# Attention and two MLP layers on one core: ten ticks per attention unit, three slots per column block, two column blocks begun early, all operands at one residue modulo 512 bytes

## The chip, the cores and the metric

The kernel runs on one core of one Trainium2 chip. The core has TensorE (PE in the profile; its weight loads are PEld), VectorE (DVE), ScalarE (ACT), GpSimd (POOL) and SyncE (SP, here only a queue for DMAs), the on-chip memory SBUF and eight PSUM banks of 128 partitions by 512 fp32 values, into which TensorE writes. The metric is the time on the device in microseconds (us), as a median over runs. Besides it there is a profile of one execution, with each instruction's start and end.

## The reference

It computes attention over 2 x 8 heads (768 positions, 64 values a head) with 4 sink positions and a window of 128, then two MLP layers on the 1536 tokens of width 512 with 2048 hidden columns.

```python
keep = is_sink | in_window
scores = np.where(keep, scale * np.matmul(q, k.transpose(0, 1, 3, 2)), -1000000000.0)
a = np.exp(scores - np.max(scores, axis=-1, keepdims=True))
a = a / (np.sum(a, axis=-1, keepdims=True) + 1e-09)
x = np.matmul(a, v)                         # -> (1536, 512)
...
r = np.maximum(x @ w_in, 0.0)               # first layer
x = (r * r) @ w_out
...
h = x @ w_in                                # second layer
P = a[0] + a[1]*h + a[2]*h*h + a[3]*h*h*h
Q = 1.0 + np.abs(b[0])*np.abs(h) + np.abs(b[1])*h*h
return (P / (Q + 1e-06)) @ w_out
```

## The kernel before

The tokens stand in four groups: 512, 256, 256 and 512 columns (GROUPS; 0 to 3). The hidden width of 2048 is worked in 16 column blocks f of 128. Every operand of a large product is split into two parts, hi and lo, and a product is three matmuls: hi by hi, hi by lo, lo by hi. So the first GEMM of a block is 4 x 3 = 12 matmuls (`gemm1`, L437 to L439, tiles xhi, xlo, whi, wlo), and the second is 8 with ghi (L460, L461; "hi matmuls" below) and 4 with glo (L464; "lo matmuls"). In the second layer the lines are L437 to L439 and L495 to L497, with yhi and ylo in place of xhi and xlo for the token tiles 0 and 2; tile 1 takes the buffers of xhi and xlo again.

Between the two GEMMs of the first layer stands `act1`: a Relu and two squares on ACT (L446 to L448) and the residual glo on DVE (L449), all in the PSUM bank that the first GEMM wrote; the bank is free when glo has been formed. The second GEMM of block f - 2 follows the first GEMM of block f (LAG = 2).

The weights come as 64-bit floats, 512 KB a load. A conversion (`w_split_`) is a cast to `top` on ACT (L134), a merge to `wt` on DVE (L135), the cast whi on ACT (L421) and the residual wlo on DVE (L422). There is one `top` buffer.

Attention works in units of two heads and two blocks of 128 positions: eight units for each of groups 0 and 3, four for each of groups 1 and 2. A unit is a generator (`att_unit`): two steps with scores (L302, "QK"; each needs two banks, whose contents DVE reduces and masks at L308, tiles p and mn, and ACT exponentiates at L310), then the sums and the normalization (L313 to L318), some empty steps, the transposes (L335, "TR", two banks, copied by ACT and DVE into pT), the sink transposes (L347, "TRs", copied by ACT into pS), then the sink products and PV (L358, L370) and a copy of the result.

The head of the program runs the eight units of group 0 one behind the other, with CONV[k] conversions at step k, and begins HEAD column blocks of the first GEMM in banks of their own as soon as a quarter of x is there. Then `group(g)` runs the layer's 16 blocks for group g, and lets the attention of group g + 1 go on beside it: `slot(k)` stands at two places in each f and calls `tick()` as often as an even spread of nt ticks asks. A tick starts a new unit if the tick's number is a multiple of PER, and moves every unit under way by one step, the new one first. In group 0 the attention has banks 6 and 7 alone, in groups 1 and 2 four banks; the first GEMM uses 4 and 5, and the second GEMM of group 0 holds 0 to 3.

TensorE's order in the head and in groups 0 to 2 is as the code writes it (`manual_schedule`); the order of the other engines, and TensorE's elsewhere, is set by a scheduler when the program is built. Each engine works through its queue in order.

Of the kernel before, what the change touches and what calls it, by code (L numbers as in the profile page):

```python
# [10 lines left out]
F32 = mybir.dt.float32  # L11
# [8 lines left out]
P = 128  # L20
# [5 lines left out]
NF = DFF // P  # L26
NC = DM // P
# [10 lines left out]
YEVAC_ACT = (0, 1)  # L38
PINNED = (0, 1, 2)
NUNIT = (4, 4, 8)  # L40
CONV = (1, 1, 1, 1, 1, 2, 2, 2, 2)
PER = 4
HEAD = 3
DEPTH = 4
NALT = 4
LAG = 2
# [1 line left out]
TAIL = 3  # L48
HP = 60
NTOP = 1  # L50
PAD = 128
IAD = 3
ST_T = 2
ST_PV = 1
TG2 = 512
GN = [sum(s[2] for s in g) * P for g in GROUPS]
# [100 lines left out]
class Fast:  # L157
# [17 lines left out]
    def setup(self):  # L175
        nc, c = self.nc, self.const
        self.zero = c.tile([P, P], BF16, name="zero")
        nc.gpsimd.memset(self.zero, 0.0)
        self.tops = [c.tile([P, WH], I32, name=f"top{i}") for i in range(NTOP)]
        self.conv_i = 0  # L180
        for top in self.tops:
            nc.gpsimd.memset(top, 0)
        self.ident = c.tile([P, P], F32, name="ident")
        self.nsw = c.tile([P, 4], I32, name="nsw")
        self.nswf = c.tile([P, 4], F32, name="nswf")
        self.par = c.tile([P, 2], F32, name="par")
        ab = c.tile([P, 6], F32, name="ab")
        self.ab = ab
        io = self.io
        nc.scalar.dma_start(self.nsw, io["nsw"].bitcast(I32).partition_broadcast(P))  # L190
        nc.scalar.dma_start(ab[:, 0:4], io["a"].partition_broadcast(P))
        nc.scalar.dma_start(ab[:, 4:6], io["bb"].partition_broadcast(P))
        make_identity(nc, self.ident)
        rel = self.wp.tile([P, WH], F32, tag="whi4_0", name="rel")[:, :P]
        col = self.wp.tile([P, WH], F32, tag="wlo4_0", name="col")[:, :P]
        nc.gpsimd.iota(rel, pattern=[[-1, P]], base=0, channel_multiplier=1,
                       allow_small_or_imprecise_dtypes=True)
        nc.gpsimd.iota(col, pattern=[[1, P]], base=0, channel_multiplier=0,
                       allow_small_or_imprecise_dtypes=True)
        v = nc.vector  # L200
        f = self.nswf
        t = c.tile([P, 2], F32, name="neg")
        v.tensor_copy(f, self.nsw)
        lo = f.rearrange("p (s w) -> p s w", w=2)[:, :, 0:1]
        hi = f.rearrange("p (s w) -> p s w", w=2)[:, :, 1:2]
        t3 = t.rearrange("p (s w) -> p s w", w=1)
        p3 = self.par.rearrange("p (s w) -> p s w", w=1)
        v.tensor_scalar(t3, lo, 0.0, 4294967296.0, op0=ALU.is_lt, op1=ALU.mult)
        v.tensor_tensor(t3, t3, lo, op=ALU.add)
        v.scalar_tensor_tensor(p3, in0=hi, scalar=4294967296.0, in1=t3, op0=ALU.mult, op1=ALU.add)  # L210
        ns, win = self.par[:, 0:1], self.par[:, 1:2]
        self.m0 = c.tile([P, P], F32, name="m0")
        self.m1 = c.tile([P, 2 * P], F32, name="m1")
        self.m2 = c.tile([P, 2 * KB], F32, name="m2")
        self.nabs = c.tile([P, 2], F32, name="nabs")
        m0, m1, m2 = self.m0, self.m1, self.m2
        tmp = lambda tag: self.wp.tile([P, WH], F32, tag=tag, name="tmp")[:, :P]
        out, fut, rel1 = tmp("whi4_1"), tmp("wlo4_1"), tmp("whi5_0")
        v.tensor_scalar(fut, rel, 0.0, -BIG, op0=ALU.is_lt, op1=ALU.mult)
        v.tensor_scalar_add(rel1, rel, 128.0)  # L220
        cur, prv = m2[:, KB : KB + P], m2[:, NSK:KB]
        v.tensor_scalar(cur, rel, win, -BIG, op0=ALU.is_ge, op1=ALU.mult)
        v.tensor_tensor(cur, cur, fut, op=ALU.min)
        v.tensor_scalar(out, col, ns, -BIG, op0=ALU.is_ge, op1=ALU.mult)
        v.tensor_tensor(m0, cur, out, op=ALU.max)
        v.tensor_scalar(prv, rel1, win, -BIG, op0=ALU.is_ge, op1=ALU.mult)
        v.tensor_tensor(m1[:, 0:P], prv, out, op=ALU.max)
        v.tensor_copy(m1[:, P : 2 * P], cur)
        v.tensor_copy(m2[:, :NSK], out[:, :NSK])
        v.tensor_copy(m2[:, KB + P :], out[:, :NSK])  # L230
        nu = 2 * sum(u[2][2] for u in units())
        self.mn = c.tile([P, nu], F32, name="mn")
        self.mn_i = 0
        c.tile([P, PAD // 4], F32, name="pad")


    def alt_tags(self, alt):
# [211 lines left out]
        nc.vector.tensor_tensor(glo, r, ghi.bitcast(F32), op=ALU.subtract)  # L449
        return ghi, glo  # L450

    def gemm2a(self, f, gg, n, acc):
        nc = self.nc
        ghi, glo = gg
        whi, wlo = self.w[(0, f, 1)]
        pk = n <= 256
        kw = dict(skip_group_check=True) if pk else {}
        for m in range(NC):
            ms = slice(m * P, (m + 1) * P)
            nc.tensor.matmul(acc[m], whi[:, ms], ghi, start=(f == 0 and not pk), stop=pk, **kw)  # L460
            nc.tensor.matmul(acc[m], wlo[:, ms], ghi, start=False, stop=pk, **kw)  # L461
        for m in range(NC):
            ms = slice(m * P, (m + 1) * P)
            nc.tensor.matmul(acc[m], whi[:, ms], glo, start=False, stop=pk or f == NF - 1, **kw)  # L464
# [35 lines left out]
    def run(self, ctx):  # L500
# [119 lines left out]

        self.att_banks = [2, 3, 6, 7, 1]
        self.new_x(0)
        hb = [self.bank(k) for k in (4, 5, 0)]
        pc = 0
        dh = []
        per = n0 // NC
# [29 lines left out]
        urgent = True  # L656
        acc, gs, ys, ysp = None, {}, {}, {}

        def second(which, g, f):
            nonlocal acc  # L660
            if f == 0 and which == 0 and GN[g] <= 256:
                bk = [self.bank(k) for k in range(2)]
# [7 lines left out]
            gg = gs.pop((which, g, f))  # L670
            if which == 0:
                n = GN[g]
                self.gemm2a(f, gg, n, acc)
                if f == NF - 1:
                    k = 0 if g == NG - 1 else g
                    y = self.yp.tile([P, self.yw[k]], F32, tag=f"y{k}", name="y")
                    if g == 2:
                        self.yx = y
                    y = y[:, : NC * n].rearrange("p (m n) -> p m n", m=NC)
                    for m in range(NC):  # L680
                        (A.copy if m % 2 == 0 or g in YEVAC_ACT else V.tensor_copy)(y[:, m], acc[m])
                    ys[g] = y
            else:
                self.gemm2b(f, gg, acc)
                if f == NF - 1:
                    for t in range(TG2 // P):
                        if g == NT2 - 1:
                            if t == 0:
                                ot = self.xp.tile([P, 4, DM], F32, tag="xhi", name="ot")
                            o = ot[:, t]  # L690
                        else:
                            o = self.stage.tile([P, DM], F32, tag="wt", name="o", bufs=2)
                        r0 = g * TG2 + t * P
                        dst = self.io["out"][r0 : r0 + P, :]
                        if g == NT2 - 1 and t == TG2 // P - 1:
                            A.copy(o[:, : DM // 2], acc[t][:, : DM // 2])
                            nc.scalar.dma_start(dst[:, : DM // 2], o[:, : DM // 2])
                            V.tensor_copy(o[:, DM // 2 :], acc[t][:, DM // 2 :])
                            nc.sync.dma_start(dst[:, DM // 2 :], o[:, DM // 2 :])
                        else:  # L700
                            (A.copy if t % 2 == 0 else V.tensor_copy)(o, acc[t])
                            nc.sync.dma_start(dst, o)
# [4 lines left out]
        def group(g):  # L707
            nonlocal sp, acc, pos, nt
            n = GN[g]
            last = g == NG - 1  # L710
            if last:
                assert done == len(us)
                sa.close()
                sp = ExitStack()
                self.ysp = mk(sp, "ysp", 1, "right")
                self.cp = self.ysp
                self.flag()
                wload(1, 3)
                nt = 0
            else:  # L720
                nt = PER * NUNIT[g] + 5
            self.att_banks = [6, 7] if n > 256 else [2, 3, 6, 7]
            pos = 0

            def slot(k):
                nonlocal pos
                while pos < min(nt, nt * (k + 2) // (2 * NF)):
                    tick()
                    pos += 1

            for f in range(NF):
                if g == 0 and f < HEAD:
                    h = hb[f]
                else:
                    h = self.gemm1(0, f, *self.x[g], n)
                gs[(0, g, f)] = self.act1(h, n)
# [1 line left out]
                    wconv(0, f + 4, 0)  # L738
                if last and f > 0:
                    wconv(1, f - 1, 0)  # L740
                slot(2 * f + 1)
                if f >= LAG:
                    second(0, g, f - LAG)
                if g == 0 and f + 1 < NF:
                    wconv(0, f + 1, 1)
                if last:
                    if f >= 3:
                        wconv(1, f - 3, 1)
                    if f in (4, 6, 8, 10):
                        with ExitStack() as cc:  # L750
                            cc.enter_context(tc.issue_after(self.lastX.ins))
                            self.split_y(0, (f - 4) // 2, ys, ysp)
                slot(2 * f + 2)
            if not last:
                while done < gdone[g + 1]:
                    tick()
# [255 lines left out]
```

## Time and profile before

| what | before |
|---|---|
| median of 3 runs | 679.44 us (678.81 to 680.25) |
| profiled execution, its own time | 680.43 us |
| its span, first to last instruction | 678.7 us |
| PE busy | 635.6 us, 94% |
| DVE busy | 424.8 us, 63% |
| ACT busy | 426.8 us, 63% |
| mean granted clock | 0.978 of full |

The head with group 0's attention runs to about 66 us, group 0 to 180, group 1 to 251, group 2 to 321 and group 3 to 405; the second layer then runs to 669. PE's busy time counts overlapping matmuls once, so 100% in a stretch means that it had a matmul in flight all the time, and not that the matmuls were as dense as they can be; how dense they are is read from their starts. A row's "idle before" is the time in which an engine had nothing in flight, with the instruction that ended it.

### The profile page before, as it was taken

How to read it: one execution, taken by the hardware profiler on the slowest of the kernel's cores; microseconds unless marked ns; L12 is line 12 of the kernel's file. 1: busy time of each engine (PE TensorE's matmuls, PEld its weight loads, DVE VectorE, ACT ScalarE, POOL GpSimd, SP SyncE). 2: the span in 40 equal slices, each digit the busy share in tenths (PEclk: the TensorE clock that was granted, in tenths of full speed). 3: DMA queues.
4: the chain of work that ended last, by engine and by line, in shares of the span. 5: the costliest groups of instructions: out<-in, count | busy, mean ns of one | idle time of the engine just before them, and what ended most of it. 6: DMA issues, size and time to landing. Idle time of an engine off the chain costs nothing.

```text
span 678.7 us, 9985 instructions
## 1 busy us (share of the span) xinstructions
PE 635.6 (94%) x3681; PEld 515.5 (76%) x3681; DVE 424.8 (63%) x849; ACT 426.8 (63%) x912; POOL 111.8 (16%) x122
## 2 busy tenths in 40 slices
PE   5668699999999999999999999999999999999994
PEld 2445467677788888899888888888888888888883
DVE  6885465543233354423666649999788887877772
ACT  4875566654455465546677758787676666766661
POOL 2111000000001011102000001353223332222221
PEclk9788699999999999999999999999999999999998
DMA  8870354432012122100455530000010000100001
GB/s 291 318 235 26 104 189 148 150 111 91 24 34 73 44 70 86 43 9 1 153 188 188 190 120 2 0 1 0 1 63 1 1 0 1 46 17 2 0 1 67
DMA packets 20794, 52.39 MB, mean 77 GB/s; under 512 B 2688, under 2 KB 8064, under 8 KB 20736
## 3 DMA queue, kind: packets, MB, share of 16 engines
q1 hardware_dynamic: 20160, 51.52, 22.3%
q8 instruction: 31, 0.51, 0.3%
q14 instruction: 27, 0.22, 0.1%
q10 hardware_dynamic: 576, 0.14, 0.1%
HBM read 48.50 MB, written 3.15 MB: 76 GB/s over the span
## 4 chain that ended last, share of the span: by engine, by line
PE 87%; ACT 6%; DVE 4%; issue 1%; DMA 1%; POOL 0%; POOLq 0%
PE b L437 13%; PE b L439 13%; PE b L438 13%; PE b L460 7%; PE b L461 7%; PE b L464 6%; PE b L496 6%; PE b L495 6%; PE b L497 6%; PE b L302 3%; ACT p L310 2%; PE b L370 2%; PE b L335 2%; ACT top L134 1%; PE b L358 1%
## 5 line engine op out<-in xcount | busy, mean ns | idle before, releaser
L437 PE MATMUL b<-xhi,whi 128*128 128x512 f32 (+1 forms) x320 | 113.7, 356 | 0.0
L439 PE MATMUL b<-xhi,wlo 128*128 128x512 f32 (+1 forms) x320 | 111.0, 347 | 0.0
L438 PE MATMUL b<-xlo,whi 128*128 128x512 f32 (+1 forms) x320 | 110.9, 347 | 0.0
L460 PE MATMUL b<-ghi,whi 128*128 128x512 f32 (+1 forms) x256 | 84.4, 346 | 6.6 <-DVE glo L449 6.6
L461 PE MATMUL b<-ghi,wlo 128*128 128x512 f32 (+1 forms) x256 | 82.9, 340 | 0.0
L486 POOL TENSOR_TENSOR glo<-t,ghi 128x512 fp32r<-128x512 f32 x34 | 45.0, 1324 | 215.3 <-ACT ghi L485 192.3
L449 DVE TENSOR_TENSOR glo<-b,ghi 128x512 fp32r<-128x512 f32 (+1 forms) x64 | 35.6, 556 | 71.2 <-ACT b L448 71.0
L496 PE MATMUL b<-wlo,ghi 128*128 128x512 f32 x192 | 74.9, 390 | 0.0
L310 ACT ACTIVATE p<-p,mn 128x288 f32<-128x288 f32 (+2 forms) x96 | 48.4, 505 | 41.6 <-DVE mn L308 41.4
L495 PE MATMUL b<-whi,ghi 128*128 128x512 f32 x192 | 74.5, 390 | 0.0
L497 PE MATMUL b<-whi,glo 128*128 128x512 f32 x192 | 72.0, 389 | 0.0
L318 POOL TENSOR_SCALAR p<-p,sums 128x288 f32<-128x288 f32 (+1 forms) x48 | 28.4, 602 | 260.8 <-DVE sums L314 179.7
L437 PEld LDWEIGHTS b<-xhi,whi 128*128 128x128 f32 x320 | 60.4, 189 | 10.3 <-issue 2.8
L439 PEld LDWEIGHTS b<-xhi,wlo 128*128 128x128 f32 x320 | 60.5, 189 | 7.7
L438 PEld LDWEIGHTS b<-xlo,whi 128*128 128x128 f32 x320 | 60.5, 189 | 7.2
L446 ACT ACTIVATE b<-b 128x512 f32<-128x512 f32 (+1 forms) x64 | 30.7, 482 | 54.9 <-PE b L439 54.7
L422 DVE TENSOR_TENSOR wlo<-wt,whi 128x512 fp32r<-128x512 f32 x64 | 45.0, 704 | 31.3 <-ACT whi L421 30.9
L308 DVE CUSTOM_DVE_ANT_0 p<-b,m 128x288 f32<-128x288 f32 (+2 forms) x96 | 37.0, 420 | 43.8 <-PE b L302 43.7
L421 ACT CAST whi<-wt 128x512 fp32r<-128x512 f32 x64 | 39.5, 617 | 31.5 <-PE b L438 21.0
L460 PEld LDWEIGHTS b<-ghi,whi 128*128 128x128 f32 x256 | 49.0, 191 | 13.1 <-DVE glo L449 7.0
L464 PE MATMUL b<-glo,whi 128*128 128x512 f32 (+1 forms) x256 | 55.6, 340 | 0.0
L461 PEld LDWEIGHTS b<-ghi,wlo 128*128 128x128 f32 x256 | 49.1, 192 | 5.1
(126 smaller groups left out, 1289.3 us busy)
## 6 DMA issues: line engine op xcount, KB each, us to landing
st<-w SPq DMA_DIRECT2D x64, 512.0 KB, 4.1
raw<-att SPq DMA_DIRECT2D x12, 400.0 KB, 3.1
rawv<-att SPq DMA_DIRECT2D x16, 192.0 KB, 2.7
raws<-att SPq DMA_DIRECT2D x16, 128.0 KB, 2.7
out<-o SPq DMA_DIRECT2D x8, 256.0 KB, 2.0
raw_e<-att SPq DMA_DIRECT2D x4, 400.0 KB, 5.4
raw<-att SPq DMA_DIRECT2D x6, 256.0 KB, 3.2
rawv<-att SPq DMA_DIRECT2D x8, 128.0 KB, 3.3
```

The costliest lines, as they stand in the source:

```text
L310: self.lastA = A.activation(p, p, AF.Exp, scale=-1.0, bias=mn, accum_out=sums[:, k * nb + i : k * nb + i + 1])
L422: nc.vector.tensor_tensor(wlo, t, whi.bitcast(F32), op=ALU.subtract)
L437: nc.tensor.matmul(h[:, :n], whi[:, cs], xhi[:, c, :n], start=(c == 0), stop=False)
L438: nc.tensor.matmul(h[:, :n], whi[:, cs], xlo[:, c, :n], start=False, stop=False)
L439: nc.tensor.matmul(h[:, :n], wlo[:, cs], xhi[:, c, :n], start=False, stop=(c == NC - 1))
L460: nc.tensor.matmul(acc[m], whi[:, ms], ghi, start=(f == 0 and not pk), stop=pk, **kw)
L461: nc.tensor.matmul(acc[m], wlo[:, ms], ghi, start=False, stop=pk, **kw)
L464: nc.tensor.matmul(acc[m], whi[:, ms], glo, start=False, stop=pk or f == NF - 1, **kw)
L486: self.lastL = nc.gpsimd.tensor_tensor(glo, t3, ghi.bitcast(F32), op=ALU.subtract)
L495: nc.tensor.matmul(acc[t], ghi[:, ts_], whi, start=(f == 0), stop=False)
L496: nc.tensor.matmul(acc[t], ghi[:, ts_], wlo, start=False, stop=False)
L497: nc.tensor.matmul(acc[t], glo[:, ts_], whi, start=False, stop=(f == NF - 1))
```

## The change

The tables of numbers:

```diff
-CONV = (1, 1, 1, 1, 1, 2, 2, 2, 2)
-PER = 4
-HEAD = 3
+CONV = (1, 1, 1, 1, 1, 1, 1, 1, 1)
+PER = 5
+HEAD = 2
...
-PAD = 128
...
-ST_T = 2
+ST_T = 5
...
-        c.tile([P, PAD // 4], F32, name="pad")
```

A unit now has three more empty steps between its normalization and its transposes (ST_T), a new one starts every fifth tick, and the head holds 9 conversions instead of 13. The removed tile of 128 bytes stood in the first pool, so every pool on the left side of SBUF moves down by 128 bytes. In the program of before the tiles whi, wlo, xhi, xlo, ghi and glo start at 96 modulo 512, and yhi and ylo, in a pool on the right side, at 480; in the changed program all of them start at 480.

The second GEMM and the slots:

```diff
-    def gemm2a(self, f, gg, n, acc):
+    def gemm2a(self, f, gg, n, acc, between):
...
+        if between:
+            between()
         for m in range(NC):
             ms = slice(m * P, (m + 1) * P)
             nc.tensor.matmul(acc[m], whi[:, ms], glo, start=False, stop=pk or f == NF - 1, **kw)
...
-        hb = [self.bank(k) for k in (4, 5, 0)]
+        hb = [self.bank(k) for k in (4, 5)]
...
-                nt = PER * NUNIT[g] + 5
+                nt = PER * NUNIT[g] + 6
...
             def slot(k):
                 nonlocal pos
-                while pos < min(nt, nt * (k + 2) // (2 * NF)):
+                first = 6 if g == 0 else -2
+                while pos < min(nt, nt * (k - first) // (3 * NF - first - 2)):
                     tick()
                     pos += 1
...
+                elif g == 0 and f == HEAD:
+                    h = self.bank(6)
+                    for c in range(NC):
+                        self.gemm1_part(0, f, c, self.x[0], n, h)
                 else:
                     h = self.gemm1(0, f, *self.x[g], n)
                 gs[(0, g, f)] = self.act1(h, n)
...
-                slot(2 * f + 1)
+                slot(3 * f + 1)
                 if f >= LAG:
-                    second(0, g, f - LAG)
+                    second(0, g, f - LAG, lambda: slot(3 * f + 2))
+                else:
+                    slot(3 * f + 2)
...
-                slot(2 * f + 2)
+                slot(3 * f + 3)
```

The new slot stands between the hi and the lo matmuls of the second GEMM. In group 0 the first tick falls on the eighth slot (f = 2), so no unit of group 1 starts in the head any more.

TensorE from the end of the head into group 0, before. L437 to L439 are the last quarter of the three column blocks in banks b4, b5 and b0, L460 is the first matmul of the second GEMM, L302 a QK burst of group 1's first unit:

```order
L302 MATMUL b6_784<-raw_700 64x288 x2
L302 MATMUL b7_785<-raw_700 64x288 x2
L437 MATMUL b4_150<-xhi_148,whi_192 128x512
L437 MATMUL b5_151<-xhi_148,whi_242 128x512
L437 MATMUL b0_152<-xhi_148,whi_308 128x512
L438 MATMUL b4_150<-xlo_149,whi_192 128x512
L439 MATMUL b4_150<-xhi_148,wlo_193 128x512
L438 MATMUL b5_151<-xlo_149,whi_242 128x512
L439 MATMUL b5_151<-xhi_148,wlo_243 128x512
L438 MATMUL b0_152<-xlo_149,whi_308 128x512
L439 MATMUL b0_152<-xhi_148,wlo_309 128x512
L460 MATMUL b0_814<-ghi_763,whi_451 128x512
```

The same place after (L345 is the sink transpose, L356 the sink product, L435 to L437 the first GEMM, L458 and L464 the hi and lo matmuls, L300 QK):

```order
L345 MATMUL b2_678<-ident_104,p_600 128x128 x2
L435 MATMUL b6_725<-xhi_147,whi_306 128x512
...
L356 MATMUL b2_678<-pS_681,raws_468 64x128 x4
...
L435 MATMUL b4_149<-xhi_147,whi_190 128x512
L435 MATMUL b5_150<-xhi_147,whi_240 128x512
L435 MATMUL b6_725<-xhi_147,whi_306 128x512
...
L437 MATMUL b6_725<-xhi_147,wlo_307 128x512
L458 MATMUL b0_753<-ghi_713,whi_446 128x512
...
L300 MATMUL b6_768<-raw_662 64x288 x2
L300 MATMUL b7_769<-raw_662 64x288 x2
L464 MATMUL b0_753<-glo_714,whi_446 128x512
```

The third column block has moved from b0 to b6, nine of its matmuls stand ahead of the sink products, and the QK bursts have left the head; the first stands between hi and lo.

TensorE in group 0, before: a QK burst of one unit and the transposes of another (L335) in the same tick, on the same two banks, after a lo matmul and ahead of the next first GEMM:

```order
L464 MATMUL b3_817<-glo_764,whi_451 128x512
L302 MATMUL b6_832<-raw_782 64x288 x2
L302 MATMUL b7_833<-raw_782 64x288 x2
L335 MATMUL b6_842<-ident_104,p_770 128x128 x4
L335 MATMUL b7_849<-ident_104,p_770 128x128 x4
L437 MATMUL b4_858<-xhi_148,whi_376 128x512
```

After, two blocks f in a row (L333 are the transposes):

```order
L437 MATMUL b4_909<-xhi_147,wlo_645 128x512
L300 MATMUL b6_939<-raw_778 64x288 x2
L300 MATMUL b7_940<-raw_778 64x288 x2
L458 MATMUL b0_753<-ghi_806,whi_787 128x512
...
L459 MATMUL b3_756<-ghi_806,wlo_788 128x512
L300 MATMUL b6_959<-raw_778 64x288 x2
L300 MATMUL b7_960<-raw_778 64x288 x2
L464 MATMUL b0_753<-glo_807,whi_787 128x512
...
L333 MATMUL b6_1018<-ident_104,p_766 128x128 x4
L333 MATMUL b7_1025<-ident_104,p_766 128x128 x4
L458 MATMUL b0_753<-ghi_873,whi_854 128x512
```

Each piece now stands alone, with at least the eight hi matmuls between it and the next on the same banks.

## Rows read from the trace of the kernel before

**Rows 1.** The page: the chain that ended last, shares of the span.

```profile
PE 87%; ACT 6%; DVE 4%; issue 1%; DMA 1%; POOL 0%; POOLq 0%
```

**Rows 2.** Busy time by stretch: window, its length, engines' busy us (instructions), clock, DMA.

```profile
72.90:78.30 5.40, 5.40 (x12) 3.79 (x12) 1.83 (x3) 1.02 (x2) 0.00 (x0) 0.50 0.57 193
78.30:180.60 102.30, 95.94 (x539) 73.62 (x539) 48.31 (x108) 58.38 (x127) 5.72 (x8) 1.00 0.35 116
251.00:320.80 69.80, 69.51 (x627) 61.48 (x626) 26.64 (x87) 37.88 (x112) 8.97 (x13) 1.00 0.13 40
```

**Rows 3.** Waits of PE from 66 to 180 us: total us, times, longest.

```profile
PE b L460 <- DVE glo L449: 6.6, 1, 6.6
PE b L335 <- DVE mn L308: 4.2, 7, 0.8
PE b L347 <- DVE mn L308: 2.2, 4, 0.6
```

**Rows 4.** Timeline of PE at group 0's start: start, us, line, operands, count, idle before.

```profile
65.89 0.39 PE L439 MATMUL b<-xhi,wlo 128*128 128x512 f32 x1
72.89 0.80 PE L460 MATMUL b<-ghi,whi 128*128 128x512 f32 x1 [6.61 <-DVE glo L449]
...
78.31 0.87 PE L302 MATMUL b<-raw 64*64 64x288 f32 x8
```

**Rows 5.** Timeline of ACT in the same wait.

```profile
67.90 0.58 ACT L447 ACTIVATE ghi<-b 128x512 fp32r<-128x512 f32 x1
...
68.89 0.59 ACT L447 ACTIVATE ghi<-b 128x512 fp32r<-128x512 f32 x1
```

**Rows 6.** Timeline of DVE: the third glo.

```profile
72.14 0.69 DVE L449 TENSOR_TENSOR glo<-b,ghi 128x512 fp32r<-128x512 f32 x1 [0.24 <-ACT b L448]
```

**Rows 7.** Timeline of PE at the end of the head.

```profile
60.78 0.38 PE L347 MATMUL b<-ident,p 128*128 128x128 f32 x2
...
61.74 0.66 PE L358 MATMUL b<-pS,raws 128*64 128x128 f32 x8
...
63.20 0.72 PE L302 MATMUL b<-raw 64*64 64x288 f32 x8
63.91 0.98 PE L437 MATMUL b<-xhi,whi 128*128 128x512 f32 x3
```

**Rows 8.** The chain that ended last, from 40 to 52 us: start, us, what.

```profile
43.51 0.78 ACT top L134
...
47.97 0.67 DVE wlo L422
```

**Rows 9.** Timeline of PE around one tick of group 0.

```profile
85.41 1.07 PE L464 MATMUL b<-glo,whi 128*128 128x512 f32 x4
86.40 0.72 PE L302 MATMUL b<-raw 64*64 64x288 f32 x8
87.68 0.44 PE L347 MATMUL b<-ident,p 128*128 128x128 f32 x2 [0.56 <-DVE mn L308]
87.87 0.48 PE L437 MATMUL b<-xhi,whi 128*128 128x512 f32 x1
88.19 0.39 PE L438 MATMUL b<-xlo,whi 128*128 128x512 f32 x1
```

**Rows 10.** Timeline of PE at group 2's start.

```profile
252.91 0.66 PE L358 MATMUL b<-pS,raws 128*64 128x128 f32 x8 [0.24 <-ACT pS L349]
```

**Rows 11.** Timeline of ACT at group 2's start.

```profile
250.89 1.18 ACT L681 COPY y<-b 128x256 f32<-128x256 f32 x4
251.93 0.57 ACT L310 ACTIVATE p<-p,mn 128x288 f32<-128x288 f32 x1
```

**Rows 12.** Timeline of PE: first matmuls of tiles 1 and 2, and tile 2's last step.

```profile
485.82 0.39 PE L437 MATMUL b<-xhi,whi 128*128 128x512 f32 x1
...
572.87 0.40 PE L437 MATMUL b<-yhi,whi 128*128 128x512 f32 x1
...
655.79 0.40 PE L437 MATMUL b<-yhi,whi 128*128 128x512 f32 x1
```

More of the change, by code (lines that the diff above doesn't have):

```diff
@@ L657, in run, with second @@
         acc, gs, ys, ysp = None, {}, {}, {}
-        def second(which, g, f):
+        def second(which, g, f, between=None):
             nonlocal acc
@@ L672, in second @@
                 n = GN[g]
-                self.gemm2a(f, gg, n, acc)
+                self.gemm2a(f, gg, n, acc, between)
                 if f == NF - 1:
```

## The prediction

> **What bounds the kernel now.** I read the page's chain of waits first: TensorE (PE) carries 87% of it [rows 1]. So a change pays where PE waits or runs at its lower clock, or where its matmuls follow each other more closely; work on other engines costs nothing while PE is fed. Next, the busy time by stretch, to see where PE has room. From 78.3 to 180.6 us (token group 0, with the attention of group 1 mixed in) PE is busy 95.94 of 102.30 us, so 6.4 us are open; from 251.0 to 320.8 it is busy 69.51 of 69.80, so nothing is open there [rows 2]. Then who PE waited for from 66 to 180 us: once 6.6 us for the residual glo, 4.2 us in 7 waits of transposes (L335) and 2.2 us in 4 waits of L347, both on the score reduction mn of VectorE (DVE) [rows 3]. These 13.0 us are what the change can reach, and I follow each in the timeline.
>
> **The start of group 0.** PE issues its last first-GEMM matmul of the head at 65.89, and the next matmul at 72.89, after 6.61 us of idle [rows 4]. In the order of before this next one writes bank b0, which holds the third column block; the bank is free when the third glo, which starts at 72.14, has read it [rows 6]. Ahead of that stand, on ScalarE (ACT), three Relu, three pairs of squares and three steps of weight conversion. The idle time has a second price: from 72.90 to 78.30 the granted clock is 0.50, the 1.2 GHz level, and twelve matmuls take 5.4 us [rows 2]. At the upper level they take 12 x 0.227 = 2.7 (0.227 us is a matmul of 512 columns: 5.441/24, from the steps of the second layer below). So 2.7 us go to the clock.
>
> After: the third block goes to bank b6, and its twelve matmuls are issued at the group's start, nine of them before the last PV of the head. I rebuild the times from rows. The sink transposes begin at 60.78 [rows 7]; 0.2 later come nine matmuls, 9 x 0.227 + 0.09 = 2.1, to 63.1. The sink products and PV took 61.74 to 63.20 = 1.46 [rows 7], so they end at 64.65. Then to the 437s it was 63.20 to 63.91, with two exponentials ahead of the xhi copy on ACT; these are gone, so I take 0.45: 65.1. Nine matmuls took 63.91 to 66.12 (65.89 + 0.23 [rows 4, 7]): PE is through at 67.3. The first block is complete at about 66.2, its Relu starts at 66.6, after two Relu and a square the first ghi is out at 68.1, and the eight hi matmuls run from 68.2 to 70.0. Then comes the catch: the first QK burst stands between hi and lo and writes b6, which the third block holds. ACT needs nine operations at 0.49 (67.90 to 68.89 is two [rows 5]) from 66.6, so to 71.0; glo and its hand-over take 72.14 to 72.89 = 0.75 [rows 4, 6]: 71.8. So PE waits 1.8 there. QK takes 0.65 and the four lo matmuls 1.0: 73.4, against 78.31 [rows 4]. That is -4.9; a second QK burst, which was done by 63.91 in the head [rows 7], is still owed, +0.65. **Start: -4.3 us.** Bounds: -6.1 if b6 is free in time; +0.4 if b6 comes 2 us later still and the clock falls again as now (2.7).
>
> **Inside the head.** Two weight conversions (of 13) leave the stretch of 41 to 48 us. On the chain they hold a top copy at 43.51, ahead of exponentials, and a wlo subtraction at 47.97, ahead of the next reduction [rows 8]; to the operations behind them it is 0.65 and 0.60 us. The third block also leaves the bursts of nine matmuls there, 0.68 us each, but exponentials on ACT cover these. I take **-1.2**, with bounds 0 (the exponentials are held by their own reductions) and -2.6 (two bursts count as well). The conversions come back in group 0, two steps of f or about 12 us ahead of their use, and that is their cover; without it each costs its 2 us of top, wt, whi and wlo.
>
> **The hand-overs.** A QK burst starts at 86.40; the L347 transpose that takes over its first bank starts at 87.68, 0.56 us of it idle [rows 9]. So the first bank comes back 1.28 us after the burst begins, 0.63 after it ends, and the second about 0.4 later: 1.05. In the order of after, a piece in group 0 is followed by at least eight matmuls, 1.81 us, before the next piece asks for either bank. The 6.4 us of waits on mn [rows 3] should go; I leave 0.5 for bursts whose second reduction stands behind a conversion on DVE: **-5.9**. Bounds: -6.4, and -3 (half survive).
>
> **What the splitting costs.** From four lo matmuls to a QK burst it is 85.41 to 86.40 = 0.99, where four matmuls are 0.91; behind a piece the first matmul takes 87.87 to 88.19 = 0.32 instead of 0.23 [rows 9]. So each excursion of PE from the GEMM into attention costs 0.08 + 0.09 = 0.17 us besides the piece. I count the excursions from group 0's first hi to the end of attention in TensorE's whole order: 45 before, 70 after, as QK and transposes no longer stand together. 25 x 0.17 = **+4.2**. In groups 1 and 2 nothing offsets it, since nothing waited there [rows 2]. Bounds: +2.5 (a piece right behind a piece paid part of this already) and +5.5.
>
> **A new tight place.** At the start of group 2 three ticks follow f = 0 at once: TR, TRs, PV, with no GEMM between. Before, a sink product there stood behind twelve matmuls and still waited 0.24 us for the pS copy [rows 10]. Now the pS copy stands on ACT behind four y copies (250.89 to 251.93 = 1.04, so 0.26 each [rows 11]), a Relu, pT and two squares: from the last lo matmul 0.2 + 1.04 + 0.26 + 0.5 + 0.52 + 0.3 + 0.15 = 3.0 us, while PE arrives after six matmuls, TR and TRs, 0.72 + 0.09 + 1.02 = 1.8. That is 1.2 instead of 0.24: **+1.0**; bounds 0 and +3. On the queue of SyncE (SP) the raws and rawv of group 1's first unit move behind four more weight loads, but the product that needs them moves three steps of f, six conversions, so I charge nothing; if they come late, the +3 holds it.
>
> **The addresses.** In the second layer the sixteen steps of token tile 1 take 485.82 to 572.87 = 87.05 us, 5.441 each; fifteen steps of tile 2 take 572.87 to 655.79 = 82.92, 5.528 each [rows 12]. No engine waits in either. What differs is the moving operand: xhi lies at 96 modulo 512 as the weights do, yhi at 480. Tiles 0 and 2 use yhi: 32 x 0.087 = **-2.8** if that is the cause, since after it all lie at 480. Bounds: 0 and -3. The Trainium skill ("TensorE: Matmul & The Clock Gate", Part 2, step 1) speaks against it: the moving operand and LDWEIGHTS have independent read ports, and loading the next weights takes nothing from the running matmul. By that rule no address matters and the sum would be -6.2. The trace shows two speeds of the same instructions, but not that the address is the cause.
>
> **Sum.** -4.3 - 1.2 - 5.9 + 4.2 + 1.0 - 2.8 = -9.0. The profiled execution took 680.43 (its span is 678.7, the rest lies around it): 671.4. It is 0.99 above the median of the runs, 679.44, and on that I put the forecast: **670.4 us**.
>
> **Rivals.** *The hand-overs fail (slower).* Two banks serve all of group 0, and conversions now stand between the two reductions of a burst on DVE, each waiting for ACT. Some 25 pieces hand over there; if each waits w, the term is 25w - 6.4 in place of -5.9 and the total 25w - 9.5: slower from w = 0.38 us. At 0.8, the longest of the waits at L335 [rows 3], it is +10.5: 689.9. Against it: 1.81 us of cover for 1.05. *The addresses do nothing:* 673.2. For it: yhi differs from xhi in its side of SBUF too, and that stays. Against it: the tile whose two residues agree is the fast one. *The start isn't mended:* ACT is late with the third block, b6 comes 2 us later and the clock falls as now, +4.7: 675.1. For it: ACT did the same nine operations with conversions between; against it: no conversion stands between them in the order of after. *Splitting is cheap and the head shrinks:* +2.5, -2.6 and -6.1 for their terms: 665.5.
>
> **How the numbers follow.** Chances: forecast 0.56 (its own range 667.5 to 673), addresses 0.14, start 0.11, cheap splitting 0.11, hand-overs 0.08. About 0.2%, 1.4 us, is what a measurement of this kernel can tell from no change. All cases but the hand-overs lie further below 679.44; of the hand-overs' 0.08 I count 0.07 as slower, and with some of the far ends of the others a tie has 0.03. Faster 0.90, same 0.03, slower 0.07. The range of 664 to 677 leaves out the hand-overs and the sums of several far ends.
>
> **What would show it.** No idle of 6 us on PE at the group's start, under 2 us before the first QK, and the clock at its upper level from there; L335 and L347 below 1 us in all among PE's waits in group 0; 5.44 us a step in all three tiles of the second layer; groups 1 and 2 longer by some 3 us together with PE busy throughout. I am wrong if PE's waits in group 0 come back under another name, if tiles 0 and 2 keep 5.53, or if groups 1 and 2 lose more than 6 us.

## The result, and the profile after

| what | before | after |
|---|---|---|
| median of 4 runs | 679.71 us (678.81 to 680.25) | 668.12 us (667.30 to 669.49) |
| profiled execution, its own time | 680.43 us | 668.77 us |
| its span | 678.7 us | 667.0 us |
| PE busy | 635.6 us, 94% | 632.6 us, 95% |
| mean granted clock | 0.978 | 0.985 |

The ratio is 0.9833 [0.9811, 0.9855]: faster, well beyond the 0.2% that can be told apart. The forecast was 670.4 us, with a range of 664 to 677. In the chain of waits PE's share rose from 87% [rows 1] to 89%:

```profile
PE 89%; ACT 4%; DVE 3%; issue 1%; DMA 1%; POOL 0%; POOLq 0%; DVEq 0%
```

To see where 11.7 us of span went, I cut both traces at the same four matmuls: the last sink transposes of the head, the matmul behind the first block's lo matmuls, and the first matmuls of groups 1 and 3. In after (the changed kernel) they are these rows of PE's timeline (start, us, line, operands, count); before has the first two in [rows 7, 4].

```profile
59.04 0.38 PE L345 MATMUL b<-ident,p 128*128 128x128 f32 x2
...
71.91 0.39 PE L435 MATMUL b<-xhi,whi 128*128 128x512 f32 x1
...
167.57 0.28 PE L435 MATMUL b<-xhi,whi 128*128 128x256 f32 x1
...
307.99 0.40 PE L435 MATMUL b<-xhi,whi 128*128 128x512 f32 x1
```

The four cuts give five stretches: the head, the start of group 0, the rest of it, groups 1 and 2, and the rest of the program. Here they are in us for the kernels of this study ("pad" is the 128 bytes, "b6" the third column block in bank b6, begun ahead of the head's last PV, "conv" the four conversions that leave the head). The start holds two QK bursts of 0.65 us in before and x1, none in x7 and x9, and one in the others.

| kernel | head | start | rest of group 0 | groups 1, 2 | rest | span |
|---|---|---|---|---|---|---|
| before | 60.78 | 17.52 | 99.40 | 139.25 | 361.69 | 678.7 |
| before without pad (x1) | 60.06 | 16.50 | 99.25 | 139.27 | 358.84 | 673.9 |
| after, b6 and conv undone (x5) | 60.69 | 15.52 | 93.02 | 140.41 | 358.84 | 668.5 |
| after, b6 undone (x2) | 59.94 | 15.67 | 93.84 | 140.41 | 358.58 | 668.4 |
| after, conv undone (x4) | 60.64 | 12.87 | 93.04 | 140.41 | 358.75 | 665.7 |
| after, old spread (x3) | 59.40 | 12.86 | 104.66 | 140.06 | 358.73 | 675.7 |
| **after** | 59.04 | 12.87 | 95.66 | 140.42 | 359.00 | 667.0 |
| after, a second profile | 58.07 | 12.84 | 95.62 | 140.40 | 358.57 | 665.5 |
| conv undone, group 0's first tick one slot later (x9) | 60.72 | 11.20 | 93.85 | 139.29 | 358.91 | 664.0 |
| conv undone, two slots later there (x7) | 60.97 | 10.35 | 94.95 | 139.28 | 358.95 | 664.5 |

The start is the stretch with the 6.61 us of idle before [rows 4]. In after PE waits twice there, 2.35 us together:

```profile
65.39 0.39 PE L437 MATMUL b<-xhi,wlo 128*128 128x512 f32 x1
66.53 0.50 PE L458 MATMUL b<-ghi,whi 128*128 128x512 f32 x1 [0.75 <-ACT ghi L445]
...
70.23 0.72 PE L300 MATMUL b<-raw 64*64 64x288 f32 x8 [1.60 <-DVE glo L447]
70.88 1.20 PE L464 MATMUL b<-glo,whi 128*128 128x512 f32 x4
```

and the clock does not fall. The busy time by stretch (window, length, busy us of PE, PEld, DVE, ACT, POOL, clock, DMA) has a granted clock of 1.00 where [rows 2] had 0.50:

```profile
66.53:71.91 5.38, 3.78 (x20) 2.49 (x21) 2.90 (x7) 3.24 (x7) 0.00 (x0) 1.00 0.00 0
71.91:170.91 99.00, 97.69 (x543) 73.57 (x541) 56.31 (x129) 67.05 (x147) 7.38 (x10) 1.00 0.48 156
```

PE's waits from 66 to 180 us, against 13.0 us in [rows 3], are 3.6:

```profile
PE b L300 <- DVE glo L447: 1.6, 1, 1.6
PE b L300 <- DVE mn L306: 1.3, 2, 1.0
PE b L458 <- ACT ghi L445: 0.7, 1, 0.7
```

The new tight place at group 2's start is there, 0.88 us of idle where [rows 10] had 0.24. On ACT the pS copy, which the sink products wait for, stands behind four y copies, a Relu, a pT copy and two squares:

```profile
235.20 1.20 ACT L681 COPY y<-b 128x256 f32<-128x256 f32 x4 [2.37 <-PE b L464]
...
237.66 0.39 ACT L347 COPY pS<-b 128x256 f32<-128x256 f32 x1
238.09 0.66 PE L356 MATMUL b<-pS,raws 128*64 128x128 f32 x8 [0.88 <-ACT pS L347]
```

In the second layer all three tiles now have the time that only tile 1 had in [rows 12]: one step of tile 0 is 448.19 - 442.75 = 5.44 us, tile 1 has 87.04/16 = 5.440, and fifteen steps of tile 2 take 81.60, 5.440 each.

```profile
442.75 0.39 PE L435 MATMUL b<-yhi,whi 128*128 128x512 f32 x1
448.19 0.39 PE L435 MATMUL b<-yhi,whi 128*128 128x512 f32 x1
475.39 0.39 PE L435 MATMUL b<-xhi,whi 128*128 128x512 f32 x1
562.43 0.39 PE L435 MATMUL b<-yhi,whi 128*128 128x512 f32 x1
644.03 0.39 PE L435 MATMUL b<-yhi,whi 128*128 128x512 f32 x1
```

### The profile page after: what moved, and what is told of

It reads as the page before. It is cut to its first block, busy times and chain, and to the rows that moved or that the text cites. A ratio compares the mean times of both kernels' runs of the same rounds, so it can differ in the third digit from the quotient of the medians.

```text
span 667.0 us, 9984 instructions
## 1 busy us (share of the span) xinstructions
PE 632.6 (95%) x3681; PEld 514.7 (77%) x3681; DVE 423.0 (63%) x849; ACT 428.4 (64%) x912; POOL 110.6 (17%) x122
## 4 chain that ended last, share of the span: by engine, by line
PE 89%; ACT 4%; DVE 3%; issue 1%; DMA 1%; POOL 0%; POOLq 0%; DVEq 0%
PE b L435 13%; PE b L436 13%; PE b L437 13%; PE b L458 7%; PE b L464 7%; PE b L496 7%; PE b L497 7%; PE b L495 7%; PE b L459 6%; PE b L300 3%; PE b L368 3%; PE b L333 2%; ACT p L308 2%; PE b L356 1%; DVE wt L134 1%
## 5 line engine op out<-in xcount | busy, mean ns | idle before, releaser
L435 PE MATMUL b<-xhi,whi 128*128 128x512 f32 (+1 forms) x320 | 113.4, 355 | 0.5 <-ACT xhi L374 0.5
L437 PE MATMUL b<-xhi,wlo 128*128 128x512 f32 (+1 forms) x320 | 111.0, 347 | 0.0
L458 PE MATMUL b<-ghi,whi 128*128 128x512 f32 (+1 forms) x256 | 84.9, 348 | 0.7 <-ACT ghi L445 0.7
L435 PEld LDWEIGHTS b<-xhi,whi 128*128 128x128 f32 x320 | 60.3, 189 | 11.9 <-issue 3.8
L437 PEld LDWEIGHTS b<-xhi,wlo 128*128 128x128 f32 x320 | 60.4, 189 | 7.6
L458 PEld LDWEIGHTS b<-ghi,whi 128*128 128x128 f32 x256 | 48.4, 189 | 12.5 <-issue 6.3
L464 PE MATMUL b<-glo,whi 128*128 128x512 f32 (+1 forms) x256 | 56.6, 343 | 0.0
L134 DVE SCALAR_TENSOR_TENSOR wt<-st,top 128x512 int32<-128x512 int32 x64 | 47.4, 741 | 7.5 <-ACT top L133 5.7
```

The source lines that it names most:

```text
L134: nc.vector.scalar_tensor_tensor(t.bitcast(I32), in0=mid, scalar=13, in1=top, op0=ALU.logical_shift_right, op1=ALU.bitwise_or)
L435: nc.tensor.matmul(h[:, :n], whi[:, cs], xhi[:, c, :n], start=(c == 0), stop=False)
L437: nc.tensor.matmul(h[:, :n], wlo[:, cs], xhi[:, c, :n], start=False, stop=(c == NC - 1))
```

## The experiments

Each ratio is against before on the same chip. The runs stand on three chips, on which before took 679.3 (x1 to x4), 680.0 (x5 to x7) and 679.4 us (x8, x9 and the second run of after), so kernels on different chips are compared by their ratios.

### The addresses alone: x1_pad_alone

Before, without the pad; everything on the left of SBUF moves down by 128 bytes.

```diff
-        c.tile([P, PAD // 4], F32, name="pad")
```

> The kernel before without its 128-byte tile, nothing else: every operand of the large products then starts at 480 modulo 512. If the residue is the cause, a step of tiles 0 and 2 of the second layer takes 5.44 us as in tile 1 (5.53 before), nothing else changes, and the profiled span falls by 2.7 to 2.8 us, to 675.9. If the changed kernel's fast tiles come from something else, the steps stay at 5.53 and the span at 678.7.

676.16 us (675.46 to 676.76), ratio 0.9955 [0.9938, 0.9971]. Fifteen steps of tile 2 take 81.60 us, 5.440 each:

```profile
569.53 0.39 PE L436 MATMUL b<-yhi,whi 128*128 128x512 f32 x1
...
651.13 0.39 PE L436 MATMUL b<-yhi,whi 128*128 128x512 f32 x1
```

From group 3 to the end it is 2.85 us less than before, the term of the addresses. The profile's other 1.9 us lie in the head (0.72) and the start (1.02), and there the two profiles differ in their granted clock. The wait for glo is 6.6 us in both, but the hi and lo matmuls behind it took 5.42 us before, at a clock of 0.50, and 4.41 here, at 0.64:

```profile
72.16:76.57 4.41, 4.41 (x13) 3.24 (x13) 1.84 (x3) 1.04 (x2) 0.00 (x0) 0.64 0.65 237
```

In the head the clock of before was 0.50 from 51.37 to 54.78 us, with PE busy for 3.08 us of it; here it was 1.00. No run shows that the pad has to do with it.

### The third block back in the head: x2_start_undone

```diff
-HEAD = 2
+HEAD = 3
-        hb = [self.bank(k) for k in (4, 5)]
+        hb = [self.bank(k) for k in (4, 5, 0)]
-                elif g == 0 and f == HEAD:
-                    h = self.bank(6)
...
```

> The changed kernel with three column blocks in the head again, the third in b0 (HEAD = 3, no block in b6). If the bank b0 and the number of blocks made the start slow, all 4.7 us between the last unit's transposes and the end of f = 2 come back. My theory is that the queue of ACT made it slow (conversions and exponentials between the squares), and that stays empty here: PE then idles some 4 us for the third glo, and what comes back is 0.3 us if the clock holds, and up to 3 if it falls to 1.2 GHz as before.

670.08 us (668.67 to 670.23), ratio 0.9856 [0.9840, 0.9873]: far less lost than the start's whole term. The wait for glo is back, at 4.5 us where before had 6.6, and with it the lower clock:

```profile
PE b L458 <- DVE glo L447: 4.5, 1, 4.5
```

The busy time from the first hi matmul to the first lo matmul:

```profile
69.62:74.50 4.88, 4.88 (x17) 2.79 (x17) 0.00 (x0) 0.00 (x0) 0.00 (x0) 0.50 0.00 0
```

So the start's term had two parts. The start is 17.52 before (16.50 in x1, where the clock rose sooner), 15.67 here and 12.87 after: 2.8 us belong to the third block. The other 0.8 to 1.9 go with what the spreading takes away there, one QK burst (0.65) and exponentials on ACT; no run isolates them. And 1.8 us of the 2.8 came back in the rest of group 0 (93.84 against 95.66), which I had not expected.

### The old spread under three slots: x3_spread_undone

```diff
-PER = 5
-ST_T = 5
-                nt = PER * NUNIT[g] + 6
+PER = 4
+ST_T = 2
+                nt = PER * NUNIT[g] + 5
```

> The changed kernel with units of seven ticks and a new one every fourth (ST_T = 2, PER = 4, nt with + 5); three slots, the start and the addresses stay. If the distance between pieces on the two banks is what took the waits away, QK and transposes stand together again, PE's waits on mn in group 0 rise from 1.3 us to 4 to 6, and the span by 2.5 to 4 us, with groups 1 and 2 up to 1 us shorter. If the emptied head and the later start of the units did it, group 0 stays at 99 us.

677.13 us (676.24 to 677.49), ratio 0.9965 [0.9951, 0.9979]: 9 us lost, more than expected, and all in group 0 (104.66 against 95.66). PE's waits from 66 to 180 us:

```profile
PE b L333 <- DVE mn L306: 5.8, 5, 3.1
PE b L345 <- DVE mn L306: 2.4, 4, 0.7
...
```

Transposes stand directly behind a QK burst again, and the longest wait costs twice: the clock is at its lower level for part of the 8 us behind it.

```profile
86.86 0.72 PE L300 MATMUL b<-raw 64*64 64x288 f32 x8
90.68 2.07 PE L333 MATMUL b<-ident,p 128*128 128x128 f32 x8 [3.10 <-DVE mn L306]
```

```profile
90.68:98.77 8.09, 7.53 (x30) 5.49 (x31) 4.82 (x11) 5.22 (x12) 0.00 (x0) 0.63 0.52 171
```

So the third slot alone does not mend group 0 (both kernels have the moved conversions); the new distances between a unit's steps are needed. Whether they would do it without the third slot, no run shows. In groups 1 and 2 the old spread is only 0.36 us shorter, with 1.7 us of waits there against 0.9 in after.

### The conversions back in the head: x4_conv_undone

```diff
-CONV = (1, 1, 1, 1, 1, 1, 1, 1, 1)
+CONV = (1, 1, 1, 1, 1, 2, 2, 2, 2)
```

> The changed kernel with 13 conversions in the head again (CONV of before). If the two conversions around 41 to 48 us are what held the head, the last unit's transposes start at about 59.8 instead of 58.0 and the span rises by 1.2 to 1.8 us. If the shorter bursts of the first GEMM (six matmuls instead of nine) did it, they stay at 58.0 and the span is within 0.5 us.

667.43 us (666.96 to 667.53), ratio 0.9822 [0.9806, 0.9839]: no loss. The median alone would say that the conversions do nothing in the head. The cuts say otherwise: the head is 1.6 us longer (60.64), and the rest of group 0 is 2.6 shorter (93.04). Part of the 1.6 is the clock. x3 has after's order in the head and, from 36 to 46 us, the same granted clock as x4; its head ends at 59.40, 1.24 us before x4's. That stretch in x3 and in x4:

```profile
36.00:46.00 10.00, 7.69 (x54) 5.24 (x55) 6.71 (x27) 5.68 (x21) 0.81 (x2) 0.66 0.57 198
36.00:46.00 10.00, 7.10 (x53) 4.85 (x54) 8.29 (x26) 7.69 (x22) 1.33 (x2) 0.66 0.84 280
```

In x4 there is no wait on mn left in group 0:

```profile
PE b L300 <- DVE glo L447: 1.6, 1, 1.6
PE b L458 <- ACT ghi L445: 0.8, 1, 0.8
```

Where after loses most of the 2.6 is seen on DVE. A QK burst is issued at 86.49, and the next matmul starts at 87.14. In after DVE does three conversion steps first and waits for ACT within them; the first reduction starts at 89.77, a conversion step follows, and PE stands at its next burst until 90.28 and, for that burst's second half, until 91.26. DVE's timeline of after, and PE's two bursts with the lo matmuls behind the second:

```profile
86.49 0.72 PE L300 MATMUL b<-raw 64*64 64x288 f32 x8
...
87.17 0.68 DVE L420 TENSOR_TENSOR wlo<-wt,whi 128x512 fp32r<-128x512 f32 x1
87.78 0.69 DVE L134 SCALAR_TENSOR_TENSOR wt<-st,top 128x512 int32<-128x512 int32 x1
89.16 0.69 DVE L420 TENSOR_TENSOR wlo<-wt,whi 128x512 fp32r<-128x512 f32 x1 [0.69 <-ACT whi L419]
89.77 0.45 DVE L306 CUSTOM_DVE_ANT_0 p<-b,m 128x288 f32<-128x288 f32 x1
...
90.14 0.69 DVE L134 SCALAR_TENSOR_TENSOR wt<-st,top 128x512 int32<-128x512 int32 x1
90.28 0.70 PE L300 MATMUL b<-raw 64*64 64x288 f32 x4 [1.03 <-DVE mn L306]
...
90.75 0.45 DVE L306 CUSTOM_DVE_ANT_0 p<-b,m 128x288 f32<-128x288 f32 x1
...
91.26 0.70 PE L300 MATMUL b<-raw 64*64 64x288 f32 x4 [0.28 <-DVE mn L306]
...
91.89 0.98 PE L464 MATMUL b<-glo,whi 128*128 128x512 f32 x3
```

In x4 the first burst starts at 88.11, one conversion step is ahead of its reductions, and they follow each other:

```profile
88.11 0.71 PE L300 MATMUL b<-raw 64*64 64x288 f32 x8
88.13 0.69 DVE L420 TENSOR_TENSOR wlo<-wt,whi 128x512 fp32r<-128x512 f32 x1 [0.69 <-ACT whi L419]
88.97 0.46 DVE L306 CUSTOM_DVE_ANT_0 p<-b,m 128x288 f32<-128x288 f32 x1
...
89.36 0.45 DVE L306 CUSTOM_DVE_ANT_0 p<-b,m 128x288 f32<-128x288 f32 x1
...
91.45 1.19 PE L464 MATMUL b<-glo,whi 128*128 128x512 f32 x4
```

From the first burst to the lo matmuls it is 91.89 - 86.49 = 5.40 us in after and 91.45 - 88.11 = 3.34 in x4. That is 2.06 of the 2.6, though the profile shows only 1.03 + 0.28 of it as idle. Set side by side, matmul by matmul, the two traces part at one more place, a QK burst at 105.87 (after), which takes 0.6 us longer without any idle shown. ACT's copy of a result (x<-b) starts at 106.00 there, behind two conversion steps, and in x4 at 104.29, ahead of them; that PE waited for this copy is not shown.

### Both undone: x5_start_conv_undone

The diffs of x2 and of x4 together.

> The kernel after with two parts undone: the third column block is no longer begun at bank b6 but in the head, at b0 (three blocks, HEAD = 3), and the four extra weight conversions stand in the head again. Two runs are behind this: the first part undone alone cost 2.8 us at the start but got 1.8 back between group 0's first lo matmuls and group 1 (span 668.4 against 667.0), the second alone cost 1.6 in the head and got 2.6 back there (665.7). Theory A (the conversions that ACT and DVE have still to do hold the first third of group 0, and whoever starts later waits less for them): what is to be got back is there once, 2.6 us, so with both undone the start's 2.8 is paid in full: span 668.5 to 669.3, and from the first lo matmuls to group 1 about 93.3 us as in the run with the second part alone undone. Theory B (the two are independent and add up): 665.7 + 1.5 = 667.2, and that stretch falls to 91.5.

670.05 us (669.77 to 670.51), ratio 0.9856 [0.9840, 0.9873]; span 668.5, rest of group 0 93.02. Theory A: with the conversions in the head there is no backlog, the later start finds nothing to get back, and the third block is worth its full 2.65 us (15.52 against 12.87). The clock is at its lower level again, for 17 matmuls in 4.86 us. At the upper level they would take about 2.5 us (an estimate: eight at 0.227 and a QK burst of 0.65), so most of the 2.65 hangs on the clock:

```profile
70.32:75.18 4.86, 4.86 (x17) 2.79 (x17) 0.00 (x0) 0.00 (x0) 0.00 (x0) 0.51 0.00 0
```

Against x1 this kernel differs by the spreading alone (and its slots): 0.9955 to 0.9856, with -6.2 in the rest of group 0, +1.1 in groups 1 and 2, -1.0 at the start and +0.6 in the head.

### Which modulus: x6_y64, x6_y256, x8_right_y64, x8_right_y256

After, with a pad of 64 or 256 bytes in the pool of yhi and ylo: as its first tile in x6, as its last in x8.

```diff
+                self.ysp.tile([P, 64 // 4], F32, name="pad")
...
+                if i == 10:
+                    self.ysp.tile([P, 64 // 4], F32, name="pad")
```

The first line is x6, the last two are x8.

> The kernel after with 64 bytes ahead of yhi and ylo in their pool on the right side of SBUF, nothing else: yhi lies at 416 modulo 512, weights and xhi at 480. Theory A (operands must agree modulo 512): tiles 0 and 2 of the second layer go back to 5.53 us a step, tile 1 stays at 5.44, span 669.8. Theory B (a smaller modulus, 64 or 32, is what counts, or the gain came from somewhere else): all three tiles at 5.44, span 667.0.

> The kernel after with 256 bytes ahead of yhi and ylo, so yhi at 224 modulo 512 and weights and xhi at 480. Theory A (modulo 512): tiles 0 and 2 at 5.53 us a step, span 669.8. Theory B (modulo 256, 128 or 64 decides): all at 5.44, span 667.0.

Spans 667.0 and 666.9, 5.44 us a step throughout. Both runs missed their aim: the pool grows from the right, the pad lay below yhi, and yhi stayed at 480 in the built programs. They only repeat after.

> The two runs x6 said nothing on addresses: in a pool that is filled from the right the first tile pushes the pool's floor down and leaves yhi where it was (480 modulo 512 in both, as the built programs show). Here 64 bytes are taken as the last tile of that pool, and yhi and ylo do lie at 416 modulo 512, weights and xhi at 480. Theory A (operands must agree modulo 512, or modulo 128): tiles 0 and 2 of the second layer at 5.53 us a step, tile 1 at 5.44, span 669.8. Theory B (agreement modulo 64 is enough): all tiles at 5.44, span 667.

> 256 bytes as the last tile of the pool on the right: yhi and ylo at 224 modulo 512, weights and xhi at 480. Theory A (modulo 512): tiles 0 and 2 at 5.53 us a step, span 669.8. Theory B (a smaller modulus, 256 or 128 or 64): 5.44 in all tiles, span 667. With the run with 64 bytes: slow there and fast here is modulo 256 or 128, slow in both is 512.

One run each, in which yhi lies at 416 and at 224. With 64 bytes the time is 671.83 us and the span 670.0: fifteen steps of tile 2 take 83.10, 5.540 each.

```profile
564.38 0.39 PE L435 MATMUL b<-yhi,whi 128*128 128x512 f32 x1
...
647.48 0.39 PE L435 MATMUL b<-yhi,whi 128*128 128x512 f32 x1
```

With 256 bytes it is 667.57 and 665.7: 81.60, 5.440 each.

```profile
561.71 0.39 PE L435 MATMUL b<-yhi,whi 128*128 128x512 f32 x1
...
643.31 0.39 PE L435 MATMUL b<-yhi,whi 128*128 128x512 f32 x1
```

The distances of 384 (before) and 448 bytes (64 down) go with 5.53 and 5.54 us a step, those of 0 and 256 with 5.44: theory A with 512 falls. Of the moduli named (512, 256, 128, 64) only 256 fits the four; with four distances tried, a rule that is no modulus is not excluded. The change's own words, modulo 512, ask for more than is needed: a distance of 256 does no harm.

### Later first ticks: x7_later_first and x9_first7

x4 with this edit, which is x9's; x7 has 8 in place of 7.

```diff
-                first = 6 if g == 0 else -2
+                first = 7 if g == 0 else 1
```

> The kernel after with the four extra conversions in the head again, and with other first steps of the spreading: group 0 begins its units two slots later (first = 8 in place of 6), groups 1 and 2 three slots later (1 in place of -2). So no QK burst stands between hi and lo of the first column block, and at group 2's start no three ticks follow each other. Theory A (the waits for b6, 1.6 us, and for the pS copy, 0.9 us, are TensorE's own and nothing else comes due): 665.7 - 2.5 = 663.2 us span, 664.9 in the median. Theory B (the same ticks over fewer slots bring pieces closer, and waits on the reduction mn return, over 1 us in group 0): 665 to 667, no gain.

x7: 666.68 us (666.27 to 667.36), ratio 0.9810 [0.9794, 0.9826], span 664.5. Between its theories: the start is 2.5 us shorter than in x4 (10.35) and groups 1 and 2 are 1.1 shorter (139.28), but the rest of group 0 is 1.9 longer (94.95), of which only 0.65 is the QK burst that was moved there. In it seven pieces of attention stand only four matmuls behind the piece before them; in after none stands fewer than eight behind.

> The kernel after with the four extra conversions in the head, group 0's spreading begun one slot later (first = 7 in place of 6, so that the first QK burst stands behind the lo matmuls of the first column block) and groups 1 and 2 three slots later (1 in place of -2). With first = 8 the start came 2.2 us sooner than with 6, but pieces right behind lo then waited some 0.4 us each and group 0 lost 1.3 us. Theory A (the lost time came from that order of pieces, and with 7 the start keeps its gain): span 663.0 to 664.0, median 665 to 666. Theory B (whatever the start gains, ACT's and DVE's backlog takes back): span 664.5 as with 8, median 666.5 to 667.

x9: 665.80 us (665.64 to 666.99), ratio 0.9805 [0.9790, 0.9819], span 664.0. The numbers fall on theory A's edge, and half of it holds. No piece of the rest of group 0 stands fewer than twelve matmuls behind another, and this stretch is 1.1 us shorter than in x7, with the same work. But the start is 0.85 us longer than in x7, as PE waits 0.69 us for glo ahead of the QK burst that now stands right behind lo. Together that is 0.25 us, and the ratios of x7 and x9 can't be told apart. x9 beats before and after. PE's waits from 66 to 180 us are down to

```profile
PE b L458 <- ACT ghi L445: 0.7, 1, 0.7
PE b L300 <- DVE glo L447: 0.7, 1, 0.7
```

> The kernel after itself, once more, beside the version with first = 7 on the same chip: 668.1 as before, ratio 0.983.

After, on the same chip as x9: 668.47 us (667.37 to 669.48), ratio 0.9840 [0.9824, 0.9855]. x9 is 2.7 us faster in the medians, and the intervals of the two ratios do not meet.

## Why the prediction was right

Its parts, against the cuts:

- **The start, -4.9 without the burst that is owed: right.** It is 17.52 to 12.87, -4.65. The wait for b6 that the rebuild found (1.8 us) is there at 1.60, and the clock stays up. What the rebuild did not tell is what does it: the third block in b6 is 2.65 us of it (x4 against x5), and the rest goes with the moved burst and with the clock: in x1, where it rose sooner, the same start is 1.0 us shorter than in before. The rival that the start isn't mended falls: idle is 2.35 us and the clock 1.00. (One sum of the rebuild, 63.1 + 1.46, makes 64.56 and not 64.65, which changes nothing.)
- **The head, -1.2: right, and for the reason given.** The head ends at 58.07 to 59.64 us in the kernels with the conversions moved and two blocks begun (seven profiles: after twice, x3, x6 and x8), and at 60.64 to 60.97 in the three with the conversions put back. At the same granted clock (0.66 from 36 to 46 us) x3 has 59.40, x6_y64 59.64 and x4 60.64, so 1.0 to 1.2 us. All four conversions were put back together; that the two on the chain do it is not shown by itself. That the bursts of nine matmuls cost nothing there holds with the conversions in the head (60.69 with three blocks, 60.64 with two); without them x2 has 59.94, one profile, and that stays open.
- **The rest of group 0: right sum, two wrong terms, so luck.** My terms there are -5.9 for the hand-overs, +0.65 for the owed burst and nine excursions of 0.17 = +1.5, together -3.7. Measured is 99.40 to 95.66, -3.74. But x5 shows -6.4 for the same spreading without the moved conversions. So the hand-overs and the splitting together gave 7.0 with the owed burst taken out, where my terms without the 0.5 for conversions make 4.9, and the moved conversions took back 2.6, where I had left 0.5. The step that failed is the price of the conversions: I gave them "two steps of f or about 12 us ahead of their use" as a cover. That covers the product that uses the weights. It does not cover the reductions that queue behind them on DVE, which I had named among the rivals and priced at 0.5. One reason for the larger gain may be that I took the waits at the idle time that the profile shows (6.4): after lost 2.06 us against x4 where it shows 1.31 of idle.
- **Splitting, +4.2: too high.** Groups 1 and 2 have 32 excursions in before and x3, 47 in after and 50 in x9, and PE's waits there are 0.5, 1.7, 0.9 and 0 us. With the waits taken off, an excursion more costs 0.03 us by x9 against before (139.29 and 139.25), 0.05 by after against before and 0.08 by after against x3; I had 0.17, read from one exit and one entry. The bound of +2.5, "a piece right behind a piece paid part of this already", is 0.10 each and was still too high; its reason fits, but no run shows it by itself.
- **The tight place at group 2, +1.0: right.** It is 0.88 us in place of 0.24 by the idle time, behind the queue on ACT that was forecast. Between x4 and x9, which takes it away together with other distances, it is 1.1.
- **The addresses, -2.8: right in size and cause**, shown by x1 and the two x8: the distance from the weights decides, not yhi's place alone. Distances of 0 and 256 bytes are free, 384 and 448 are not. The rule of the Trainium skill that I had weighed ("TensorE: Matmul & The Clock Gate", Part 2, step 1: independent read ports, so that a weight load takes nothing from the running matmul) would have had x8_right_y64 at 5.44 us a step. It took 5.54, and the measurement decides; by which path the address acts is not shown.

So the total came within 2.3 us of the forecast. In the rest of group 0 two errors of 2.1 us cancel: hand-overs and splitting came out better than forecast, the moved conversions worse. What is left is mostly the 2.4 us by which groups 1 and 2 were charged too high. By the ratios, one part after the other: addresses -3.1 us (x1), spreading -6.7 (to x5), third block -2.3 (to x4), conversions +0.7 (to after). Each is uncertain by 1 to 2 us, so the last can't be told from nothing there.

## What to carry to other kernels

Price a moved piece of work by every queue that it enters: these conversions were early enough for their own reader and still held up DVE's reductions, for which TensorE waited. A median that shows no effect can hide two that cancel; cut the traces at the same instructions before an edit is called idle. Putting distance between producer and consumer on TensorE, even at the price of more switches, paid in group 0, where hand-overs were on the path; the switches cost 0.03 to 0.08 us each.

## What the runs showed of the hardware that was not expected

- Matmuls with yhi or ylo as the moving operand start 232 to 234 ns apart, in place of 226 to 227, when the operand lies at a distance of 384 or 448 bytes modulo 512 from the weights; at 0 and 256 there is nothing to see.
- Behind an idle stretch of 4.5 us on PE the granted clock was at 0.50 for the next 4.9 us (x2), and after a wait of 3.10 us it averaged 0.63 over 8.1 us (x3); with waits of 0.75 and 1.60 it stayed at 1.00 (after). Behind the same wait of 6.6 us it was 0.50 over 5.4 us in before and 0.64 over 4.4 us in x1.
- From the first block's lo matmuls on the program repeats closely: the rest of group 0 took 95.62 to 95.66 us in the six profiles that share after's order there, groups 1 and 2 140.40 to 140.42. The head varied by 1.6 us among the same kernels, and most of the scatter that the profiles show lies there. It goes with the granted clock: from 36 to 46 us this was 0.83 in the two shortest heads (58.07 and 58.39) and 0.61 to 0.66 in the other four (59.04 to 59.64).
